# Three moves in the opening lists of an attention and expert kernel: k of two pairs, V's copies and loads, a subtraction

## The chip, the core and the metric

The kernel runs on one core of a Trainium2 chip. A core has five engines, each with an instruction queue of its own that is worked off in order: TensorE (PE in the profile; PEld is its weight load), VectorE (DVE), ScalarE (ACT), GpSimd (POOL) and SyncE (SP, which only requests transfers). Sixteen DMA engines carry out transfers that SyncE, ScalarE and GpSimd request. The metric is the time of one launch on the device in microseconds (us), as the median of several runs.

## What is computed

Block-causal attention of 8 batches with 8 heads, 576 rows, 64 columns, and then a layer of 8 experts of which each row takes one. Cut to what matters here:

```python
scores = (1/sqrt(D)) * q @ k.T                 # q, k, v: 8 x 8 x 576 x 64, float32
scores = where(block_i >= block_j, scores, -1e9)   # blocks of 64 rows
attn = exp(scores - max(scores)); attn /= sum(attn) + 1e-9
x = (attn @ v), as 4608 rows of 512
# second stage: logits = x @ w_gate, argmax, at most `capacity` (80) rows for an expert,
# out[rows] = gate * (relu(x[rows] @ w1[e]) @ w2[e])
```

## The kernel before

The attention works on 32 pairs of heads, two heads of one batch at a time, so that the two fill 128 partitions. A pair goes through these steps, which are methods of `Pair`:

- `load` requests q (on SyncE), `load_k` requests k: four transfers of 72 KB on GpSimd's queue (L577), for pairs 2 and up. `load_v` requests V in three transfers on GpSimd's queue (L587, L590) and two small ones on SyncE's.
- `prep(0)` turns q: VectorE transposes it in blocks of 32 (L623) and GpSimd multiplies the result `T0` by 1/8 (L626). `prep(1)` turns k into `T1`, with no scaling. For pair 0 TensorE does this instead.
- `scores` lets TensorE multiply `T0` and `T1` into PSUM, in three goes: "3" (two PSUM tiles, 512 and 64 columns), "2" (448 and 64) and "10" (320 and 192). The rows by which the prediction counts time are the x8 products of L645.
- `max` takes the negated row maxima on VectorE (L681), `less` subtracts the maxima of the last block there (L685), and `soft` exponentiates on ScalarE (L702, and L694 for the last block).
- `back` turns the exponentials with TensorE (L732, L740), `take` copies them out of PSUM, mostly on ScalarE (L789), `pad` copies V into a tile with zeros (GpSimd, L599), and `values` multiplies with V on TensorE (L781, L759).

The order of all this is written by hand. `TURN` is a list of steps for iteration i; an entry `(d, what, ...)` does step `what` of pair i + d. `OPENING` holds other lists for the iterations -2, -1 and 0; iteration 1 and all later ones took `TURN`. The lists set the order of emission, and so the place of each instruction in its engine's queue. So `scores` "2" of pair 3 is emitted in iteration 2, and the `prep(0)` that feeds it in iteration 1. Buffers: four for q, four for k, four for V, two for each of `T0` and `T1`, four PSUM tiles that go round.

Two more facts that the emission order decides. Where two engines read the same PSUM tile, the one whose read is emitted later waits for the other's. And a transfer requested by GpSimd carries a wait for the landing of the one eight places ahead of it on that queue.

The second stage, from about 290 us, is ordered by a scheduler that works with simulated times; there TensorE multiplies gathered rows with the experts' weights (L1121). Two small products (L1072, L1086) check the choice of rows; a register load of `bad_i` on SyncE reads the outcome.

Of the kernel before, what the change touches and what calls it, by code (L numbers as in the profile page):

```python
# [34 lines left out]
TURN = (  # L35
    (1, "begin"),
    (0, "scores", "3"),
    (-3, "flip"),
    (0, "max", 3, 0),
    (-1, "back", "C"),  # L40
    (1, "scores", "2"),
    (-1, "take", "back", "C"),
    (0, "max", 3, 1),
# [45 lines left out]
OPENING = {  # L89
    -2: (  # L90
        (2, "prep", 0),
        (2, "load_v"),
        (2, "prep", 1),
        (6, "load"),
    ),
    -1: (
        (1, "begin"),
        (1, "scores", "2"),
        (1, "max", 2, 1),
        (1, "max", 2, 0),  # L100
        (1, "max", 4),
        (1, "soft", 2, 1),
        (1, "soft", 2, 0),
        (1, "less"),
        (1, "soft", 4),
        (6, "load"),
    ),
    0: (
        (0, "scores", "3"),
        (0, "max", 3, 1),  # L110
        (0, "max", 3, 0),
        (0, "scores", "10"),
        (1, "prep", 0),
        (1, "prep", 1),
        (3, "load_k"),
        (1, "begin"),
        (1, "scores", "2"),
        (0, "soft", 3, 1),
# [14 lines left out]
        (1, "soft", 4),  # L133
        (2, "prep", 0),
        (1, "load_v"),
        (4, "load_k"),
        (0, "pad"),
        (2, "load_v"),
        (0, "sum"),
# [5 lines left out]
        (0, "take", "back", "A"),  # L145
    ),
}


@with_exitstack  # L150
# [1264 lines left out]
```

## Time and profile before

| what | us |
|---|---|
| median of 3 timed runs | 407.41 (407.29 to 409.0) |
| the profiled execution | 412.18 |
| its span, first to last instruction | 410.5 |
| TensorE busy | 381.6 (93% of the span) |
| VectorE, ScalarE, GpSimd busy | 280.5, 264.8, 253.9 |

A profile shows one execution. The rows further down are of three kinds: lines of its page, groups of waits, and the timeline of one engine, where consecutive instructions of one kind are merged into a row with its start, its length and, in brackets, how long the engine had stood idle before and what ended that.

### The profile page before, as it was taken

The page shows a single profiled execution, that of the slowest core. Times are in us where ns is not written, and L with a number is a line of the kernel's source. Part 1 is how long each engine was busy: PE and PEld are TensorE (multiplying, and loading weights), DVE is VectorE, ACT ScalarE, POOL GpSimd, SP SyncE. Part 2 cuts the span into 40 slices and gives each one's busy share as a digit, 9 for nine tenths or more (in the row PEclk, how much of TensorE's full clock was granted, in tenths as well). Part 3 has the DMA queues.
Part 4 walks back from the last instruction along what each step waited for, and adds up shares of the span by engine and source line. Part 5 has one row for each costly group of instructions (what it writes and reads, how often), then busy time and mean ns, then how long its engine had stood idle before and what let it go on. Part 6 is the DMA issues. An engine that isn't in the chain of part 4 may idle for free.

```text
span 410.5 us, 15557 instructions
## 1 busy us (share of the span) xinstructions
PE 381.6 (93%) x6351; PEld 295.5 (72%) x6351; DVE 280.5 (68%) x651; ACT 264.8 (65%) x700; POOL 253.9 (62%) x440
## 2 busy tenths in 40 slices
PE   7887999999999999999999999999785999999990
PEld 3565777777777776777777776777544999999980
DVE  5774998998998999899899899887652131111120
ACT  2793999899898999999999999987031111110100
POOL 7598786898798798799779978721587010000000
PEclk9996999999999999999999999999998899999996
DMA  9999639879897997998989999996829999899300
GB/s 142 147 159 144 124 87 233 200 157 191 220 193 154 187 218 156 204 212 158 221 187 222 235 263 330 304 322 217 274 84 255 314 301 317 293 324 314 126 19 22
DMA packets 120124, 84.46 MB, mean 206 GB/s; under 512 B 94429, under 2 KB 96477, under 8 KB 120048
## 3 DMA queue, kind: packets, MB, share of 16 engines
q1 hardware_dynamic: 102432, 45.55, 48.4%
q0 software_dynamic: 15808, 37.55, 36.4%
q8 instruction: 52, 0.85, 0.9%
q10 hardware_dynamic: 1808, 0.31, 0.5%
q14 instruction: 24, 0.20, 0.2%
HBM read 63.25 MB, written 20.33 MB: 204 GB/s over the span
## 4 chain that ended last, share of the span: by engine, by line
PE 84%; POOL 4%; issue 3%; DVE 3%; DMA 2%; SPq 1%; ACT 0%; POOLq 0%; ACTq 0%; DVEq 0%
PE sc L645 23%; PE sc L781 21%; PE ps L1121 11%; PE sc L732 10%; PE av L1121 8%; PE sc L403 2%; PE sc L740 2%; PE sc L422 1%; POOL ld L577 1%; POOL vn L590 1%; PE pm L1164 1%; DMA P<-in_k_dram 1%; PE pm L1134 1%; DMA ld<-in_q_dram 1%; PE sc L759 1%
## 5 line engine op out<-in xcount | busy, mean ns | idle before, releaser
L702 ACT ACTIVATE P<-sc,negm 128x448 f32<-128x448 f32 (+3 forms) x256 | 146.0, 584 | 15.7 <-DVE negm L681 12.3
L681 DVE TENSOR_REDUCE negm<-sc 128x1 f32<-128x448 f32 (+4 forms) x224 | 127.0, 616 | 15.2 <-PE sc L652 13.6
L645 PE MATMUL sc<-T,T 64*128 64x64 f32 (+4 forms) x768 | 113.5, 420 | 7.1 <-POOL T L626 6.4
L645 PEld LDWEIGHTS sc<-T,T 64*128 64x128 f32 x768 | 71.8, 190 | 39.3 <-issue 25.3
L577 POOL DMA_DIRECT2D ld<-in_k_dram x120 | 81.9, 688 | 0.1
L789 ACT COPY PT<-sc 128x1024 f32<-128x1024 f32 x63 | 60.8, 1016 | 13.3 <-PE sc L732 12.6
L781 PE MATMUL sc<-PT,vn 128*64 128x128 f32 (+1 forms) x512 | 61.0, 380 | 0.6 <-ACT PT L789 0.6
L1169 POOL DMA_INDIRECT out_dram<-y,si x8 | 7.5, 933 | 77.4 <-DVE y L1165 57.2
L732 PE MATMUL sc<-ident,P 64*128 64x64 f32 x1280 | 53.6, 227 | 0.1
L702 ACT ACTIVATION_READ_ACCUMULATOR P<-sc,negm 128x1 f32 x256 | 53.0, 207 | 0.0
L781 PEld LDWEIGHTS sc<-PT,vn 128*64 128x64 f32 x512 | 33.9, 138 | 23.5 <-issue 22.3
L1121 PE MATMUL ps<-xsT,w 128*64 128x80 f32 x1024 | 43.5, 242 | 4.6 <-issue 4.6
L732 PEld LDWEIGHTS sc<-ident,P 64*128 64x128 f32 x1280 | 45.2, 138 | 3.0 <-ACT P L702 1.0
L623 DVE STREAM_TRANSPOSE T<-ld 128x576 f32<-128x576 f32 x62 | 47.3, 764 | 0.0
L1121 PEld LDWEIGHTS ps<-xsT,w 128*64 128x64 f32 x1024 | 40.3, 143 | 7.2 <-issue 6.6
L626 POOL TENSOR_SCALAR T<-T 128x576 f32<-128x576 f32 x31 | 20.7, 668 | 37.6 <-DVE negm L681 18.7
L590 POOL DMA_DIRECT2D vn<-in_v_dram x64 | 39.8, 628 | 0.2 <-DMA w<-in_moe_w_dram 0.2
L1146 ACT ACTIVATE hT<-ps 128x320 f32<-128x320 f32 x16 | 7.0, 438 | 48.1 <-PE ps L1121 48.1
L1156 DVE COPY yT<-av 128x320 f32<-128x320 f32 x7 | 3.4, 491 | 50.0 <-PE av L1121 50.0
L1121 PE MATMUL av<-hT,w 128*64 128x80 f32 x896 | 32.7, 233 | 0.0
L791 DVE COPY xT<-sc 128x576 f32<-128x576 f32 x32 | 24.0, 750 | 12.0 <-PE sc L759 12.0
L1121 PEld LDWEIGHTS av<-hT,w 128*64 128x64 f32 x896 | 32.0, 137 | 0.0
(191 smaller groups left out, 523.8 us busy)
## 6 DMA issues: line engine op xcount, KB each, us to landing
w<-in_moe_w_dram SPq DMA_DIRECT2D x48, 512.0 KB, 5.4
out_dram<-zero SPq DMA_DIRECT2D x18, 512.0 KB, 8.2
ld<-in_q_dram SPq DMA_DIRECT2D x124, 72.0 KB, 4.1
ld<-in_k_dram POOLq DMA_DIRECT2D x120, 72.0 KB, 4.4
xs<-Y POOLq DMA_DIRECT2D x28, 288.0 KB, 5.5
vn<-in_v_dram POOLq DMA_DIRECT2D x32, 128.0 KB, 5.1
vn<-in_v_dram POOLq DMA_DIRECT2D x64, 64.0 KB, 4.9
w<-in_moe_w_dram POOLq DMA_DIRECT2D x8, 512.0 KB, 9.1
```

Of the source, the lines that this page charges most:

```text
L577: eng.dma_start(self.nat[x][r], (q, k)[x][self.b, self.h0 + h, :, 32 * i:32 * i + 32] .rearrange("(g r) d -> r g d", r=32))
L590: nc.gpsimd.dma_start(self.vn[c * BLK:(c + 1) * BLK, 1], turned[:, :, 1 - c])
L623: nc.vector.transpose(t, self.nat[x].rearrange("p g d -> p (g d)"))
L626: nc.gpsimd.tensor_scalar(t, t, scalar1=SCALE, scalar2=1.0, op0=ALU.mult, op1=ALU.mult)
L645: nc.tensor.matmul(to[h], lhsT=self.T[0][r, q:q + P], rhs=self.T[1][r, k0:k1], start=start, stop=stop)
L681: nc.vector.tensor_reduce(to, src, axis=AX.X, op=ALU.max, negate=True)
L702: nc.scalar.activation(dst, src, AF.Exp, bias=self.negm[0:n, u, h:h + 1], scale=1.0, accum_out=self.bt.sums[0:n, u, self.h0 + h:self.h0 + ...
L732: nc.tensor.transpose(pt[:, c, to(c, n_)], row[u][r, h, k(u, h, j):k(u, h, j) + P], ident[r, r])
L781: nc.tensor.matmul(to, lhsT=lhs, rhs=rhs, start=(n_ == 0), stop=(n_ == len(steps) - 1))
L789: nc.scalar.copy(*self.out.pop((what, x)))
L791: nc.vector.tensor_copy(*self.out.pop((what, x)))
L1121: yield nc.tensor.matmul(dst(b)[64 * c:64 * (c + 1)], lhsT=w_[:, a, col:col + 64], rhs=x_[:, a], start=(a == 0 and b == 0), stop=(a == n - ...
```

## The change

Three lists change. In `OPENING[-1]` the subtraction `less` of pair 0 is emitted ahead of two exponentials that read the same PSUM tile, where it had come behind them. In `OPENING[0]` the request of k of pair 3 goes from behind `prep(1)` of pair 1 to the head of the list, and the request of k of pair 4 from behind V's request of pair 1 to the place that k of pair 3 had. And iteration 1 gets a list of its own: `TURN` with `pad` of pair 1 and `load_v` of pair 3 moved from ahead of `prep(0)` of pair 3 to behind it.

```diff
--- before.py
+++ after.py
@@ -99,20 +99,21 @@
         (1, "max", 2, 1),
         (1, "max", 2, 0),
         (1, "max", 4),
+        (1, "less"),
         (1, "soft", 2, 1),
         (1, "soft", 2, 0),
-        (1, "less"),
         (1, "soft", 4),
         (6, "load"),
     ),
     0: (
+        (3, "load_k"),
         (0, "scores", "3"),
         (0, "max", 3, 1),
         (0, "max", 3, 0),
         (0, "scores", "10"),
         (1, "prep", 0),
         (1, "prep", 1),
-        (3, "load_k"),
+        (4, "load_k"),
         (1, "begin"),
         (1, "scores", "2"),
         (0, "soft", 3, 1),
@@ -133,7 +134,6 @@
         (1, "soft", 4),
         (2, "prep", 0),
         (1, "load_v"),
-        (4, "load_k"),
         (0, "pad"),
         (2, "load_v"),
         (0, "sum"),
@@ -145,6 +145,9 @@
         (0, "take", "back", "A"),
     ),
 }
+_put = [step for step in TURN if step not in ((0, "pad"), (2, "load_v"))]
+_at = _put.index((2, "prep", 0)) + 1
+OPENING[1] = tuple(_put[:_at]) + ((0, "pad"), (2, "load_v")) + tuple(_put[_at:])
 
 
 @with_exitstack
```

On GpSimd's queue, in the opening (`ld1` is k, `vn` V, `T0` q turned; L577 requests k, L626 scales q). Before, `T0_297` being pair 1's:

```order
L369 MEMSET sums_250 64x8
L626 TENSOR_SCALAR T0_297<-T0_297 128x576
L577 DMA ld1_302<-in_k_dram 32x18x32 x4
L626 TENSOR_SCALAR T0_352<-T0_352 128x576
L587 DMA vn_355<-in_v_dram 128x4x64
```

and now:

```order
L372 MEMSET sums_250 64x8
L580 DMA ld1_272<-in_k_dram 32x18x32 x4
L629 TENSOR_SCALAR T0_302<-T0_302 128x576
L580 DMA ld1_307<-in_k_dram 32x18x32 x4
L629 TENSOR_SCALAR T0_357<-T0_357 128x576
```

k of pair 3 (`ld1_302` before, `ld1_272` now) stands ahead of the scaling of pair 1's q, and k of pair 4 has the place that it left.

On the same queue, from there to the scaling of pair 3's q (`T0_486` before, `T0_478` now; L599 is V's copy). Before:

```order
L587 DMA vn_355<-in_v_dram 128x4x64
L590 DMA vn_355<-in_v_dram 64x4x64 x2
L577 DMA ld1_361<-in_k_dram 32x18x32 x4
L599 COPY VZ_133<-vn_222 64x256 x2
L587 DMA vn_368<-in_v_dram 128x4x64
L590 DMA vn_368<-in_v_dram 64x4x64 x2
L577 DMA ld1_394<-in_k_dram 32x18x32 x4
L599 COPY VZ_133<-vn_355 64x256 x2
L587 DMA vn_455<-in_v_dram 128x4x64
L590 DMA vn_455<-in_v_dram 64x4x64 x2
L626 TENSOR_SCALAR T0_486<-T0_486 128x576
```

and now:

```order
L590 DMA vn_360<-in_v_dram 128x4x64
L593 DMA vn_360<-in_v_dram 64x4x64 x2
L602 COPY VZ_133<-vn_222 64x256 x2
L590 DMA vn_368<-in_v_dram 128x4x64
L593 DMA vn_368<-in_v_dram 64x4x64 x2
L580 DMA ld1_394<-in_k_dram 32x18x32 x4
L629 TENSOR_SCALAR T0_478<-T0_478 128x576
L602 COPY VZ_133<-vn_360 64x256 x2
L590 DMA vn_483<-in_v_dram 128x4x64
L593 DMA vn_483<-in_v_dram 64x4x64 x2
```

Between the scalings of pair 2's and of pair 3's q stand four groups (V of pair 1, a copy, V of pair 2, k of pair 5) where there were seven; k of pair 4, the copy of pair 1's V and V of pair 3 no longer stand there.

The queues of VectorE, ScalarE and SyncE keep their order through the attention. On VectorE and ScalarE the waits move: before, the subtraction L685 of pair 0 waited for ScalarE's exponentials; now the first of these waits for the subtraction.

In the second stage the scheduler sets a few instructions otherwise. TensorE, in expert 2's first layer (`ps`<-`xsT`,`w` are its products, `ones` the checking products), before:

```order
L1121 MATMUL ps_5860<-xsT_5617,w_4753 64x80 x13
L1072 LDWEIGHTS ones_110
L1072 MATMUL av_5810<-chk_5802,ones_110 128x10
L1164 MATMUL pm_5850<-ident_79,yT_5766 80x128 x4
L1121 MATMUL ps_5860<-xsT_5617,w_4753 64x80 x19
L1121 MATMUL ps_5894<-xsT_5617,w_4753 64x80 x7
L1086 LDWEIGHTS ones_110
L1086 MATMUL av_5823<-dsb_5819,ones_110 128x1
L1121 MATMUL ps_5894<-xsT_5617,w_4753 64x80 x25
```

and now:

```order
L1124 MATMUL ps_5860<-xsT_5617,w_4753 64x80 x9
L1075 LDWEIGHTS ones_110
L1075 MATMUL av_5810<-chk_5802,ones_110 128x10
L1167 MATMUL pm_5850<-ident_79,yT_5766 80x128 x4
L1124 MATMUL ps_5860<-xsT_5617,w_4753 64x80 x15
L1089 LDWEIGHTS ones_110
L1089 MATMUL av_5823<-dsb_5819,ones_110 128x1
L1124 MATMUL ps_5860<-xsT_5617,w_4753 64x80 x8
L1124 MATMUL ps_5894<-xsT_5617,w_4753 64x80 x32
```

The first checking product stands four products earlier, the second fifteen. On VectorE there, before:

```order
L1109 TENSOR_TENSOR xn_6172<-xg_5452 80x4x64 x2
L1094 TENSOR_SCALAR comb_5495<-ids_5793 80x8
L1056 TENSOR_TENSOR comb_5495<-comb_5495,gsum_5795 80x8
L1074 TENSOR_SCALAR good_5812<-av_5810,iota_p_113,caplt_124 80x8
L1084 TENSOR_REDUCE nb_5821<-av_5810 128x1
L1078 SCALAR_TENSOR_TENSOR dif_5814<-occ_5800,caplt_124,good_5812 80x8
L1165 TENSOR_SCALAR y_5849<-pm_5850,comb_5495 80x512
L1080 TENSOR_REDUCE dsum_5817<-dif_5814 128x1
L1082 SCALAR_TENSOR_TENSOR dsb_5819<-cap_123,dsum_5817 128x1
```

and now:

```order
L1097 TENSOR_SCALAR comb_5495<-ids_5793 80x8
L1059 TENSOR_TENSOR comb_5495<-comb_5495,gsum_5795 80x8
L1112 TENSOR_TENSOR xn_6172<-xg_5452 80x4x64 x2
L1077 TENSOR_SCALAR good_5812<-av_5810,iota_p_113,caplt_124 80x8
L1087 TENSOR_REDUCE nb_5821<-av_5810 128x1
L1081 SCALAR_TENSOR_TENSOR dif_5814<-occ_5800,caplt_124,good_5812 80x8
L1083 TENSOR_REDUCE dsum_5817<-dif_5814 128x1
L1085 SCALAR_TENSOR_TENSOR dsb_5819<-cap_123,dsum_5817 128x1
L1168 TENSOR_SCALAR y_5849<-pm_5850,comb_5495 80x512
```

The scaling of `y` has moved behind `dsb`, which the second checking product reads, and the division `xn` behind two short operations. On SyncE the register load of `bad_i` stands six weight transfers later.

## Rows read from the trace of the kernel before

**Rows 1.** The page's chain of work that ended last: share of the span by engine.

```profile
PE 84%; POOL 4%; issue 3%; DVE 3%; DMA 2%; SPq 1%; ACT 0%; POOLq 0%; ACTq 0%; DVEq 0%
```

**Rows 2.** TensorE's waits, 20 to 45 us: line, releaser, us in total, times, longest.

```profile
PE sc L645 <- POOL T L626: 3.8, 1, 3.8
```

**Rows 3.** Timeline of TensorE: start us, us, line, operation, out<-in, count, [idle before].

```profile
14.87 1.19 PE L645 MATMUL sc<-T,T 64*128 64x448 f32 x8 [1.78 <-POOL T L626]
...
27.42 1.25 PE L645 MATMUL sc<-T,T 64*128 64x512 f32 x8
...
28.80 0.41 PE L740 MATMUL sc<-ident,P 64*128 64x64 f32 x5
33.05 2.18 PE L645 MATMUL sc<-T,T 64*128 64x448 f32 x8 [3.84 <-POOL T L626]
...
35.10 2.06 PE L645 MATMUL sc<-T,T 64*128 64x320 f32 x8
...
41.57 1.25 PE L645 MATMUL sc<-T,T 64*128 64x512 f32 x8
...
43.30 1.19 PE L645 MATMUL sc<-T,T 64*128 64x448 f32 x8
...
49.39 1.25 PE L645 MATMUL sc<-T,T 64*128 64x512 f32 x8
```

**Rows 4.** Busy time of each engine by stretch, granted clock, DMA share, GB/s.

```profile
31.00:33.00 2.00, 0.00 (x0) 0.00 (x0) 0.00 (x0) 0.56 (x2) 1.92 (x5) 0.57 1.18 157
33.00:35.00 2.00, 1.95 (x8) 1.13 (x10) 0.00 (x0) 0.00 (x0) 2.00 (x4) 0.50 1.29 156
...
39.00:41.00 2.00, 2.00 (x50) 1.75 (x48) 1.25 (x5) 1.64 (x8) 1.53 (x3) 1.00 0.56 101
```

**Rows 5.** Timeline of GpSimd, opening, columns as in Rows 3.

```profile
6.02 2.91 POOL L577 DMA_DIRECT2D ld<-in_k_dram  x4
...
14.14 0.68 POOL L626 TENSOR_SCALAR T<-T 128x576 f32<-128x576 f32 x1 [3.04 <-DVE T L623]
...
19.28 0.81 POOL L587 DMA_DIRECT2D vn<-in_v_dram  x1
...
21.32 2.67 POOL L577 DMA_DIRECT2D ld<-in_k_dram  x4
...
26.78 2.66 POOL L577 DMA_DIRECT2D ld<-in_k_dram  x4
29.48 0.84 POOL L599 COPY VZ<-vn 64x256 f32<-64x256 f32 x2
...
32.34 0.66 POOL L626 TENSOR_SCALAR T<-T 128x576 f32<-128x576 f32 x1
32.96 2.73 POOL L577 DMA_DIRECT2D ld<-in_k_dram  x4
```

**Rows 6.** Timeline of VectorE, opening.

```profile
11.65 0.28 DVE L685 TENSOR_TENSOR P<-sc,negm 64x128 f32<-64x128 f32 x1 [1.48 <-ACT P L702]
...
13.18 1.42 DVE L623 STREAM_TRANSPOSE T<-ld 128x576 f32<-128x576 f32 x2
...
24.85 0.77 DVE L623 STREAM_TRANSPOSE T<-ld 128x576 f32<-128x576 f32 x1
...
26.51 0.76 DVE L791 COPY xT<-sc 128x576 f32<-128x576 f32 x1 [0.22 <-PE sc L759]
27.18 0.77 DVE L623 STREAM_TRANSPOSE T<-ld 128x576 f32<-128x576 f32 x1
```

**Rows 7.** Timeline of ScalarE, the copies ahead of pair 3's first product.

```profile
27.12 1.93 ACT L789 COPY PT<-sc 128x1024 f32<-128x1024 f32 x2
```

**Rows 8.** Requests of tile ld, 0 to 50 us: from issue to landing.

```profile
DMA to landing us min/median/max: 4.1/4.7/5.8
```

**Rows 9.** Timeline of TensorE, second stage, up to the second checking product.

```profile
333.86 2.02 PE L1121 MATMUL ps<-xsT,w 128*64 128x80 f32 x52
335.81 0.18 PE L1086 MATMUL av<-dsb,ones 128*128 128x1 bf16 x1
```

**Rows 10.** Timeline of VectorE there, what the second product reads.

```profile
333.97 0.75 DVE L1165 TENSOR_SCALAR y<-pm,comb 80x512 f32<-80x512 f32 x1
...
334.82 0.16 DVE L1082 SCALAR_TENSOR_TENSOR dsb<-cap,dsum 128x1 bf16<-128x1 f32 x1
```

## The prediction

> **What bounds the kernel now.** I read first the chain of work that ended last: TensorE holds 84% of it, every other engine 4% or less [rows 1]. So the question is where TensorE stands still or runs slowly, and whether the change touches that place. The waits of TensorE in the opening hold one that counts, 3.8 us in one piece, for GpSimd's scaling of a turned q [rows 2]. TensorE's timeline places it: the products of pair 2 and the turning of pair 1 end at 28.80 + 0.41 = 29.21, and pair 3's "2" product starts at 33.05, after 3.84 us of nothing [rows 3]. The granted clock falls in that pause, to 0.57 of full speed between 31 and 33 us, and is 0.50, the lower of the two levels (1.2 GHz), between 33 and 35, with TensorE at work again; by 39 us it is back at 1.00 [rows 4]. That product takes until 35.10 there, 2.05 us; the next pair's same rows run at the upper level with 1.19 for the merged row against 2.18 [rows 3].
>
> The price of the whole disturbance is read without splitting it: from one pair's "3" product to the next it is 41.57 - 27.42 = 14.15 us, and in the next, undisturbed turn 49.39 - 41.57 = 7.82 us [rows 3]. That is **6.33 us** too many: 3.84 of pause and 2.49 of slow clock and what hung on it. From 41.57 on the chain is TensorE without a break of this size, so a microsecond won here should reach the end.
>
> **Why GpSimd is late.** GpSimd scales pair 3's q at 32.34 [rows 5], though VectorE had turned it by 24.85 + 0.77 = 25.62 [rows 6]. It is not waiting: from 19.28 on it works through requests of V and k and V's copies, and none of the rows up to there has idle time in brackets.
>
> **The change, part by part.**
>
> *Three groups leave the stretch ahead of that scaling.* k of pair 4 takes from 21.32 for 2.67; the copy of pair 1's V and the request of pair 3's V take from 29.48 to 32.34, 2.86 us [rows 5]. Together 5.53. The scaling then starts at 32.34 - 5.53 = 26.8, behind the transpose (25.62), and ends 0.66 later at 27.5. TensorE wants it at 29.21, so 1.7 us of slack take the place of 3.84 of lateness. What is late next at 29.21? The turned k of pair 3 is there at 27.18 + 0.77 = 27.95 [rows 6]. The PSUM tile is freed by ScalarE's second copy at 27.12 + 1.93 = 29.05 [rows 7]. Both just make it. ScalarE and VectorE then have the lead that they have in an undisturbed turn. So the pause goes, and the clock, whose fall came in the pause, has no reason to fall: -6.33 us.
>
> *What comes behind the scaling.* The groups are not removed; they are now ahead of pair 4's scaling. GpSimd from 26.8: scaling 0.62 (32.34 to 32.96), copy and V 2.86, k of pair 6 2.73, a copy 0.84, V 2.04 (19.28 to 21.32) [rows 5]; that is 35.9, and with its own 0.66 pair 4's scaling ends at 36.6. TensorE will want it at 43.30 - 6.33 = 36.97 [rows 3]. Cover: 0.4 us. After that GpSimd gains on TensorE, since its turn is 0.62 + 2.73 + 0.84 + 2.04 = 6.2 us against 7.82. I cost it at nothing; if the cover is gone, every tenth beyond 0.4 is lost, up to the length of a k group, 2.7 us, less 0.4.
>
> *k of pair 3 in GpSimd's pause.* GpSimd stands idle from 11.10 to 14.14 for VectorE's transpose of pair 1's q; a k group has taken 2.66 to 2.91 us [rows 5]. Put there it ends at 13.8 to 14.0, ahead of 14.14. TensorE's first product of pair 1 hangs on that scaling, after 1.78 us of waiting at 14.87 [rows 3], and all that follows hangs on that product, so lateness here is paid in full. The risk is the wait for landings: the second to fourth request need pair 2's first three, issued between 6.02 and 8.2. Landings took 4.1 to 5.8 us, median 4.7 [rows 8]. Counted from the end of an issue, 5.8 would put the last request at 14.0 to 14.7 and the scaling 0.56 later than now; counted from its start, nothing is held. I take no delay (the median), and keep +0.56.
>
> *The subtraction.* Before, VectorE stood idle 1.48 us until 11.65 for ScalarE's exponentials [rows 6]. Now the subtraction can run at 10.17, and the maxima and transposes behind it move up by as much: pair 1's q is turned at about 12.5 in place of 13.9. The exponentials, now behind the subtraction, start some 0.28 later, its length, but ScalarE waits again for VectorE behind them. Alone this would bring pair 1's scaling forward by 1.4; but k of pair 3 now fills GpSimd until 13.8. What is left is 14.14 - 13.8 = 0.34 us at best. I take 0.1 us of gain for this part and the one before together, from bounds of -0.34 to +0.56.
>
> *k of pair 4 earlier.* It is requested near 14.8 in place of 21.3 and used far behind; no path. It joins transfers in a stretch in which the DMA share is above 1.1 [rows 4], so landings may lengthen; V of pair 1, requested at 19.28 as before, is copied at about 27.4 in place of 29.48, and has six us in place of eight, against a longest landing of 5.8 [rows 8]. SyncE's queue is passed by nothing.
>
> *The second stage.* The second checking product stands 15 products earlier. The 26 products of the list ahead of it are 52 in the trace and took from 333.86 to 335.81, so 75 ns each [rows 9]: it is reached 1.1 us earlier, at 334.7. What it reads ended at 334.82 + 0.16 = 334.98, but 0.67 of that was the scaling of `y` ahead of it, from 333.97 to the next start [rows 10], now behind: 334.3. No wait. The register load is later on a queue in which weights follow; it can hold nothing that it did not hold before. Nought, and at most 0.3 either way.
>
> Sum: -6.33 - 0.1 = **-6.4 us**. The profiled execution's 412.18 would become 405.8 (span 410.5 to 404.1). The median of the timed runs lies 4.77 below the profiled time; the pause is made by the order of one queue, so I take it to be in the timed runs too: 407.41 - 6.4 = **401.0**.
>
> **A rule that speaks against it.** k groups took the same time with VectorE at rest (2.73 at 32.96, VectorE 0.00 busy [rows 4, 5]) as beside a copy out of PSUM and a transpose (2.66 at 26.78 [rows 5, 6]). The Trainium skill, page "SBUF — State Buffer", section "SBUF: two separate sides", says that VectorE in its two-port modes locks GpSimd out, so that a transfer requested there cannot be written out until VectorE is done. By the next section of that page of the Trainium skill a request of about 620 ns then takes some 3100. The rows show no lengthening by what VectorE runs here; a copy from SBUF to SBUF beside a request is not among them.
>
> **Rivals.**
> 1. *Pair 4's scaling becomes the late one.* For: cover of 0.4 us only, landings that can hold a request or V's copy. Against: no such hold in the trace before. A lateness of 1 to 2.5 us costs 0.6 to 2.1: 401.6 to 403.1; as one figure 402.3.
> 2. *The clock is not won back.* The pause goes but another short stop keeps the lower level, or the timed runs never fell to it: only 3.84 is gained: 403.6. Against: the stop of 1.78 us at 14.87 is followed by a product of 1.19, the upper level's length [rows 3].
> 3. *The change does little of what it says in timed runs.* The 4.77 us between profiled and timed could be this very pause, made long by profiling. Then 6.4 - 4.77 = 1.6 is left: 405.8, within 0.5%.
> 4. *Slower: k of pair 3 holds pair 1's scaling.* Its four requests, 0.69 us each in the trace, become long in their new place beside VectorE's transposes. The delay d is paid once, and with a further 2.49 once TensorE's stop of 1.78 there grows to the 3.84 that went with a fallen clock. Break-even is d = 6.33 - 2.49 = 3.84; it is slower by 2.04 us from d = 5.88 on, a group of 3.04 + 5.88 = 8.9 us, 2.2 a request. At 2.3: a group of 9.2, d = 6.16, 407.41 + 6.16 - 3.84 = 409.7. Against: 2.66 to 2.91 for every group, whatever VectorE did [rows 5].
>
> By the 3100 ns of the Trainium skill's page "SBUF — State Buffer" the group would take 12.4 us and the sum would be some 413, an estimate from that page alone.
>
> **How the numbers follow.** Forecast 0.66 (400.3 to 401.6), rival 1 0.13, rival 2 0.09, rival 3 0.08, rival 4 0.04. The range reaches from a gain of 6.33 + 0.34 + 0.3, and 0.2 for the spread of timed runs, 400.2, up to rival 2 with its neighbours, 403.9; it leaves out rivals 3 and 4. A measurement of this kernel can tell about 0.5%, 2.04 us, from no change. Faster by more: forecast and rivals 1 and 2, 0.88; within: rival 3, 0.08; slower: 0.04.
>
> **What would show it.** In the changed profile TensorE's wait for GpSimd of 3.8 us is gone, the granted clock is 1.00 from 29 to 41 us, pair 3's scaling starts near 26.8, pair 4's ends within 0.4 us of TensorE's need, "3" products follow each other by 7.8 us from 27 us on, and the end comes 6.4 us earlier. A k group over 3 us at 11.1, a scaling of pair 1 after 14.2, or a stop of TensorE near 37 us would show steps wrong; an opening shorter by 6 us with an end that is not would show that the chain breaks later.

## The result and the profile of the changed kernel

The changed kernel took 406.39 us, median of eleven runs (403.18 to 408.05); the kernel before took 411.21 in eleven runs taken with them (407.29 to 413.92). The ratio is 0.9893 with a 95% interval of 0.9853 to 0.9934. It was timed three more times in the experiments below, each time beside the kernel before: 0.9832 [0.9777, 0.9887], 0.9859 [0.9801, 0.9917] and 0.9848 [0.9781, 0.9916]. Ratios here and below are taken without the slowest runs of either kernel (over 1.5% above its fastest), so they can differ a little from the quotient of the medians. The four, weighted by the inverse squares of their intervals, give 0.9865 with about 0.0026 either way: 1.35%, or 5.5 us of 411. The forecast was 401.0, a ratio of 0.9843 to the 407.41 from which it set out. So the sign was right, the gain 0.9 us smaller than forecast, and the time itself 2.5 us above the upper end of the range, 403.9, since its starting point was wrong.

The profiled execution took 406.74 us (span 404.9, mean granted clock 0.986); before it was 412.18 (410.5, 0.975).

TensorE's timeline, opening, x8 products of L648 (before L645): start, length, idle before in brackets.

```profile
14.53 1.19 PE L648 MATMUL sc<-T,T 64*128 64x448 f32 x8 [1.41 <-POOL T L629]
...
27.08 1.25 PE L648 MATMUL sc<-T,T 64*128 64x512 f32 x8
...
28.82 1.19 PE L648 MATMUL sc<-T,T 64*128 64x448 f32 x8
...
34.91 1.25 PE L648 MATMUL sc<-T,T 64*128 64x512 f32 x8
...
37.17 1.19 PE L648 MATMUL sc<-T,T 64*128 64x448 f32 x8 [0.47 <-POOL T L629]
...
38.23 1.11 PE L648 MATMUL sc<-T,T 64*128 64x320 f32 x8
...
43.27 1.25 PE L648 MATMUL sc<-T,T 64*128 64x512 f32 x8
```

Against [rows 3]: the pause of 3.84 us ahead of pair 3's "2" product is gone (28.82, no bracket) and the product takes 1.19 in place of 2.05. The next "3" product comes at 34.91 in place of 41.57, 6.66 earlier. One pair on, TensorE waits 0.47, and of the gain 6.12 is left (43.27 against 49.39).

Busy time by stretch, columns as in [rows 4]; the figure third from the end is the granted clock.

```profile
31.00:33.00 2.00, 2.00 (x24) 1.28 (x24) 2.00 (x4) 1.90 (x8) 2.00 (x4) 1.00 0.82 162
33.00:35.00 2.00, 2.00 (x62) 1.93 (x58) 1.75 (x6) 1.87 (x9) 1.90 (x4) 1.00 1.14 151
```

The clock stays at the upper level where it was 0.57 and 0.50. GpSimd's timeline, against [rows 5]:

```profile
11.05 2.67 POOL L580 DMA_DIRECT2D ld<-in_k_dram  x4
13.79 0.68 POOL L629 TENSOR_SCALAR T<-T 128x576 f32<-128x576 f32 x1
...
23.77 1.36 POOL L580 DMA_DIRECT2D ld<-in_k_dram  x2
25.97 1.33 POOL L580 DMA_DIRECT2D ld<-in_k_dram  x2 [0.85 <-DMA vn<-in_v_dram]
27.38 0.66 POOL L629 TENSOR_SCALAR T<-T 128x576 f32<-128x576 f32 x1
28.00 0.84 POOL L602 COPY VZ<-vn 64x256 f32<-64x256 f32 x2
...
36.46 0.67 POOL L629 TENSOR_SCALAR T<-T 128x576 f32<-128x576 f32 x1
```

k of pair 3 fits into the pause (11.05 + 2.67 = 13.72) and pair 1's scaling follows at 13.79. Pair 3's scaling starts at 27.38 in place of 32.34. Ahead of it the third request of k of pair 5 stood still for 0.85 us until a part of V had landed, the transfer eight places ahead on the queue. So pair 4's scaling ends at 37.13, and TensorE, which wanted it at 36.70, waits.

VectorE, with the subtraction ahead of the exponentials (before, 11.65 with 1.48 of waiting, [rows 6]):

```profile
10.24 0.28 DVE L688 TENSOR_TENSOR P<-sc,negm 64x128 f32<-64x128 f32 x1
10.44 1.40 DVE L684 TENSOR_REDUCE negm<-sc 128x1 f32<-128x576 f32 x2
11.77 1.42 DVE L626 STREAM_TRANSPOSE T<-ld 128x576 f32<-128x576 f32 x2
```

From 43 us the two timelines run alike, shifted by 6.12, up to the 29th "3" product at 244.51 (before, 250.63). Then TensorE's timeline shows this:

```profile
244.51 1.25 PE L648 MATMUL sc<-T,T 64*128 64x512 f32 x8
...
249.40 1.20 PE L648 MATMUL sc<-T,T 64*128 64x448 f32 x8 [3.09 <-POOL T L629]
...
250.45 2.06 PE L648 MATMUL sc<-T,T 64*128 64x320 f32 x8
...
257.40 1.30 PE L648 MATMUL sc<-T,T 64*128 64x512 f32 x8
```

It waits 3.09 us for a scaling, and the clock falls behind the wait: the 64x320 product takes 2.06 in place of 1.11. This interval is 12.89 us long where before it was 8.92, with a wait of 0.75. Of the gain 2.15 is left behind it. From the last "3" product to the end of the span the changed kernel's profile is shorter again, 130.02 against 133.46. The experiments show that neither of these two differences can be laid to the change from one profile.

The chain that ended last, share of the span by engine, against [rows 1] with 84% of TensorE and 2% of transfers:

```profile
PE 76%; DMA 10%; POOL 6%; issue 3%; DVE 2%; ACT 0%; POOLq 0%; ACTq 0%; DVEq 0%
```

Of the 10%, 6% are three landings of weights and V between 215 and 244 us, which reach TensorE by way of GpSimd's queue; the rest lies at the start of the second stage, 12.36 us of it in one transfer that ScalarE requested. In the third and fourth profile of the changed kernel the share of transfers is 14% and 4%.

In the second stage TensorE reached the second checking product without a wait, as forecast; what it reads had ended at 326.62 + 0.16 = 326.78.

```profile
327.47 0.18 PE L1089 MATMUL av<-dsb,ones 128*128 128x1 bf16 x1
```

```profile
326.62 0.16 DVE L1085 SCALAR_TENSOR_TENSOR dsb<-cap,dsum 128x1 bf16<-128x1 f32 x1
```

### The profile page after: what moved, and what is told of

The parts are those of the page before. It is cut to its first block, busy times and chain, and to the rows that moved or that the text cites. A ratio compares the mean times of both kernels' runs of the same rounds, so it can differ in the third digit from the quotient of the medians.

```text
span 404.9 us, 15556 instructions
## 1 busy us (share of the span) xinstructions
PE 378.3 (93%) x6351; PEld 292.2 (72%) x6351; DVE 280.9 (69%) x651; ACT 264.6 (65%) x700; POOL 254.3 (63%) x440
## 4 chain that ended last, share of the span: by engine, by line
PE 76%; DMA 10%; POOL 6%; issue 3%; DVE 2%; ACT 0%; POOLq 0%; ACTq 0%; DVEq 0%
PE sc L648 21%; PE sc L784 19%; PE ps L1124 11%; PE sc L735 10%; PE av L1124 8%; DMA vn<-in_v_dram 4%; DMA xs<-rs 3%; DMA w<-in_moe_w_dram 2%; POOL ld L580 2%; PE sc L406 2%; PE sc L743 1%; PE pm L1167 1%; PE sc L425 1%; POOL vn L593 1%; PE pm L1137 1%
## 5 line engine op out<-in xcount | busy, mean ns | idle before, releaser
L648 PE MATMUL sc<-T,T 64*128 64x64 f32 (+4 forms) x768 | 112.5, 417 | 5.7 <-POOL T L629 5.0
L648 PEld LDWEIGHTS sc<-T,T 64*128 64x128 f32 x768 | 71.3, 188 | 37.5 <-issue 24.8
L626 DVE STREAM_TRANSPOSE T<-ld 128x576 f32<-128x576 f32 x62 | 47.3, 765 | 0.0
L1124 PE MATMUL ps<-xsT,w 128*64 128x80 f32 x1024 | 40.1, 234 | 1.4 <-issue 1.4
L1124 PEld LDWEIGHTS ps<-xsT,w 128*64 128x64 f32 x1024 | 37.2, 137 | 3.6 <-issue 2.8
```

Of the source, the lines that this page charges most:

```text
L626: nc.vector.transpose(t, self.nat[x].rearrange("p g d -> p (g d)"))
L648: nc.tensor.matmul(to[h], lhsT=self.T[0][r, q:q + P], rhs=self.T[1][r, k0:k1], start=start, stop=stop)
L1124: yield nc.tensor.matmul(dst(b)[64 * c:64 * (c + 1)], lhsT=w_[:, a, col:col + 64], rhs=x_[:, a], start=(a == 0 and b == 0), stop=(a == n - ...
```

## The experiments

Three readings are taken from every profile: the start of the sixth "3" product (the opening), the interval behind the 29th (the place near 250 us), and the stretch from the last "3" product to the end of the span. What lies between them can be left out: from the sixth "3" product to the 29th all profiles but the two with weights spread take 193.40 to 193.45 us, and from the 30th to the last all twenty take 17.43 to 17.50. An interval is named by the product that ends it: the fourth is the one from the third to the fourth "3" product.

### Both kernels again

Both unchanged, in a later set of runs.

> The kernel before, unchanged, against itself: ratio 1.000. Theory A (the opening's gain of 6.1 us is whole, and what is missing is scatter of places late in the program): its profile repeats the opening to 0.1 us (14.15 us between the third and fourth "3" products, GpSimd wait 3.8 us) and differs from the first profile by up to some us behind 245 us, that is in the products around pair 29 and in the second stage; runs scatter by 2 us or more. Theory B (the later stages give back 1.5 us of the gain by themselves, because they are bound by transfers): the late places of this profile look like those of the first one to about 0.5 us.

> The changed kernel again. Theory A: opening as in its first profile (third to fourth "3" product 7.8 us, a wait of 0.5 us at pair 4), GpSimd's lateness near 245 us another size than 3.1 us, ratio to before 0.985 (6.1 us) within its interval. Theory B: the wait near 245 us is again about 3 us where the kernel before has 0.8, and the ratio is 0.989 (4.5 us).

Measured: the kernel before 410.97 us, 1.0031 [0.9989, 1.0073] of itself; the changed kernel 404.36, 0.9832 [0.9777, 0.9887]. Readings: 56.94, 10.20 and 131.66 before; 51.30, 11.84 and 129.36 changed. At the sixth product both are within 0.3 us of the first pair of profiles. The kernel before came there another way: the clock fell early, behind the stop ahead of pair 1's first product (0.53 of full speed between 17 and 19 us), so its first interval was 10.68 in place of 9.57, and the interval with the pause was 13.30 in place of 14.15. The three runs of 407.29 to 409.0, on which the forecast stood, were the low end of a scatter: they are the three lowest of eleven, the other eight being 409.55 to 413.92, and the profiled 412.18 lies in the midst of these. Three runs picked out of eleven by chance are the three lowest once in 165 times, so they look like a set of their own. Profiling adds nothing that shows: in the eighteen runs of the experiments the profiled execution lies 0.2 us above the median on average, from 3.05 below it to 3.01 above.

### Each part alone

The list of iteration 1 alone:

```diff
+_put = [step for step in TURN if step not in ((0, "pad"), (2, "load_v"))]
+_at = _put.index((2, "prep", 0)) + 1
+OPENING[1] = tuple(_put[:_at]) + ((0, "pad"), (2, "load_v")) + tuple(_put[_at:])
```

> Only V's copy and request behind the scaling of q in iteration 1. By the queue of GpSimd: pair 3's scaling at 29.5 in place of 32.3, so TensorE waits 1.0 us in place of 3.8, with no fall of the clock; pair 4's scaling then ends at 39.2 where TensorE wants it at 38.0, a wait of 1.2; gain 4.05 us at pair 4. If the lateness of pair 3 alone counted (no carrying over to pair 4), 5.3 us.

The requests of k alone (`load_k` of pair 3 to the head of `OPENING[0]`, of pair 4 in its place):

```diff
     0: (
+        (3, "load_k"),
...
-        (3, "load_k"),
+        (4, "load_k"),
...
-        (4, "load_k"),
```

> Only k of pairs 3 and 4 moved. By the queue of GpSimd: pair 3's scaling at 29.7, TensorE waits 1.2 us, no fall of the clock, pair 4's scaling in time, gain 5.1 us; with the list of iteration 1 alone it is more than the whole, so the parts overlap. If the moves were additive, this part would be 6.1 less the 4 of the other, 2 us.

The subtraction alone (`less` of pair 0 ahead of the two `soft` in `OPENING[-1]`):

> Only the subtraction of pair 0 ahead of the two exponentials. VectorE's stop of 1.5 us at 10.2 goes; pair 1's q is turned at 12.5 and scaled from 12.7, since no k request stands ahead of it here, so TensorE's first product of pair 1 starts at 13.5 in place of 14.9. GpSimd's queue and the stop of TensorE at pair 3 move as one: gain 1.3 us, stop and slow clock unchanged. If the exponentials, now behind the subtraction, set the pace, no more than 0.3 us.

Measured: 0.9853 [0.9803, 0.9904], 0.9868 [0.981, 0.9925] and 0.9955 [0.9914, 0.9996]. At the sixth "3" product (57.23 in the first profile of before) they start at 53.75, 54.75 and 56.05: 3.5, 2.5 and 1.2 us earlier, where 4.05, 5.1 and 1.3 had been worked out. The subtraction came out as forecast, and alone it leaves the pause whole (3.80). The other two fell short for causes that the rows show. With the list alone the waits for pair 3's and pair 4's scaling came as worked out, 1.00 and 1.15 us, but TensorE's stop ahead of pair 1's first product, no longer than before (1.78, [rows 3]), was followed by a slow product:

```profile
14.76 1.86 PE L648 MATMUL sc<-T,T 64*128 64x448 f32 x8 [1.78 <-POOL T L629]
```

The granted clock between 15 and 17 us was 0.53 there and 1.00 in the kernel before. The third "3" product came at 28.00 in place of 27.42, and these 0.58 us are what the gain fell short by. It is not the list's doing, since the second profile of the kernel before has such a fall behind the same stop. With the requests alone, k of pair 5 stood still 0.91 us for a landing, pair 3's scaling came at 30.64, and TensorE waited:

```profile
26.30 1.44 POOL L577 DMA_DIRECT2D ld<-in_k_dram  x2 [0.91 <-DMA vn<-in_v_dram]
...
30.64 0.66 POOL L626 TENSOR_SCALAR T<-T 128x576 f32<-128x576 f32 x1
```

```profile
31.36 1.19 PE L645 MATMUL sc<-T,T 64*128 64x448 f32 x8 [2.21 <-POOL T L626]
```

The wait of 2.21 cost 11.74 - 7.83 = 3.91 us in all, since the clock fell to 0.50 between 33 and 35. So no part alone takes the pause away; together they do. My 5.1 for the requests alone had left the landing wait out and the clock with it.

The times do not separate the parts. The list alone and the requests alone stand 6.0 and 5.4 us below the kernel before, with 2.1 and 2.4 either way, about what the whole change gains (5.5 over four sets of runs, 6.9 in this one). That is 2.6 and 3.0 more than their openings show, and what it is was not shown.

### Is the loss near 250 us the new order's? Scaling first in all iterations, weights requested elsewhere

```diff
-OPENING[1] = tuple(_put[:_at]) + ((0, "pad"), (2, "load_v")) + tuple(_put[_at:])
+TURN = tuple(_put[:_at]) + ((0, "pad"), (2, "load_v")) + tuple(_put[_at:])
```

> The changed kernel with V's copy and request behind the scaling of q in every iteration from 1 on, not in iteration 1 alone. Theory G (in the changed kernel some 3 us more than before are lost near pair 29, where GpSimd, held by the landings of weights that it requested, scales q late): the scaling stands 2.9 us earlier there, so the interval that was 12.9 and 11.8 us falls to 8 to 9, and the wait of 0.5 us at pair 4 goes too; 3 to 5 us faster than the changed kernel, about 401. Theory N (the interval near pair 29 is long for another reason, a late k or V, or chance): 0.5 us faster.

Measured: 0.9846 [0.9785, 0.9907]; 51.04, 12.68, 129.38. With the scaling ahead of V's copy and load in every turn the interval stays as long, so the order of these groups is not what makes it, and the 3 to 5 us expected did not come.

The next two spread the sixteen early parts of the weights (ten requests, the last two of four parts each), one in each of iterations 10 to 25 (`EARLY` had 2, 2, 2, 2, 4, 4 in iterations 24 to 29), in the changed kernel and in the one before:

```diff
-    EARLY = {n - 8: 2, n - 7: 2, n - 6: 2, n - 5: 2, n - 4: 4, n - 3: 4}
+    EARLY = {i: 1 for i in range(n - 22, n - 6)}
```

> The changed kernel with the weights that GpSimd requests ahead of the second stage spread, one of 16 parts in each of the iterations 10 to 25, in place of 2 to 4 parts in iterations 24 to 29. Theory G: no landing holds GpSimd near pair 29, that interval falls to 8 to 9 us, 3 to 4 us faster than the changed kernel, and 6 us faster than the kernel before with the same spread. Theory N: the interval stays at 12, no gain, or the holding moves to iterations 10 to 25.

> The kernel before with the same spread of weights. Theory G: its interval near pair 29 falls from 8.9 and 10.2 to 8 to 9, so it gains 0.5 to 2 us, less than the changed kernel does; the two then differ by the 6.1 us of the opening. Theory N: the two differ by what they differ now, 4.5 to 6 us, with the interval near pair 29 as it is.

Measured: 0.9897 [0.9836, 0.9957] and 1.0035 [0.999, 1.008], no better than without the edit. The interval behind the 29th product falls to 8.33 and 8.34, but the loss moves to where the weights are now requested: in the changed kernel four intervals of 9.54 to 11.56, with waits of TensorE for GpSimd's scaling of 1.09, 1.65 and 0.94 us between 190 and 229 us, and in the one before four of 9.97 to 12.24, where other profiles have 8.3 to 8.9. The long interval goes with the requests of weights.

### Fewer transfers near 250 us, and the changed kernel a third time

The 512 KB transfers that set `out` to zero were requested in iterations 5 to 27 without every fourth; now in 4 to 21, one in each.

```diff
-            if 4 <= i < n - 4 and i % 4:
+            if 4 <= i < 4 + nz:
```

> The changed kernel, with the 18 transfers that set out to zero (512 KB each, SyncE) requested in iterations 4 to 21, one in each, in place of iterations 5 to 27 without every fourth. In the changed kernel three of them are requested at 224.9, 234.0 and 237.0 us, in the stretch in which GpSimd's requests stand still for landings of weights, k and V. Theory L (the gain is lost near 250 us because GpSimd's requests wait for landings among too many transfers): without these 1.5 MB in that stretch the interval between 3-products there falls from 11.8 to 12.9 to at most 9.5, TensorE's wait there from 2 to 3 us to under 1, and the time from about 405 to 402 to 403. Theory M (what is lost there depends on the weights' own rate alone; the clears take nothing from it): interval 11.5 or more, time 404.5 or more. If the earlier stretch is spoiled by the closer transfers, intervals between 60 and 200 us grow beyond 7.8 to 8.9.

> The kernel before with the same earlier transfers of zeros. Theory L: the loss of 1 to 2.3 us in the interval near 250 us goes, time 409 to 409.5 against 410.5, and the difference to the changed kernel with the same edit is 6 to 6.5 us, the opening's whole gain. If the difference stays at 4.5 to 5 us, the gain is lost behind 260 us as well.

> The changed kernel once more, beside the two others on the same chip: 404 to 406 us, opening as before (3-products 4 to 6 near 34.9, 43.4, 51.2), interval near 250 us 11 to 13 if the larger loss there belongs to the changed kernel; 9 to 10.5, as in the kernel before, if it was scatter of landings.

Measured: 0.9847 [0.9794, 0.99], 1.0018 [0.9982, 1.0053], 0.9859 [0.9801, 0.9917]. Readings: 51.37, 10.30, 133.73; 57.28, 13.68, 133.72; 51.62, 9.02, 134.16. Taking the zeros out of that stretch made no difference that shows. But two profiles settle another question. In the changed kernel, unchanged:

```profile
247.68 1.19 PE L648 MATMUL sc<-T,T 64*128 64x448 f32 x8 [0.85 <-POOL T L629]
```

and in the kernel before with earlier zeros:

```profile
256.33 1.88 PE L645 MATMUL sc<-T,T 64*128 64x448 f32 x8 [3.78 <-POOL T L626]
```

The changed kernel has the short interval (9.02, as 8.92 in the first profile of before), and the order of before has the longest of all (13.68). So the loss near 250 us is not the change's own: it is there in both, the interval being 0.6 to 5.3 us longer than the 8.34 that later runs show for it without a wait.

### The weights off GpSimd's queue; k of pair 5 behind the scaling

The ten early requests of weights go to SyncE, in the changed kernel and in the one before:

```diff
-            nc.gpsimd.dma_start(w_[:, a], view[:, a])
+            nc.sync.dma_start(w_[:, a], view[:, a])
```

> The changed kernel with the early transfers of weights (ten requests at 215 to 256 us) requested by SyncE in place of GpSimd. Theory W: near 250 us TensorE waits for GpSimd's scaling because requests on GpSimd's queue wait for the landing of weights eight places ahead (landings of 6.5 to 14 us). Then with the weights off this queue the holds fall from 4 to 6 us in all to under 2, pair 28's scaling is in time, the interval is 8.3 to 8.9 in place of 9.0 to 12.9, and the time is 1 to 4 us below the changed kernel's. Rival: the transfers themselves are too slow there (the DMA share is above 1.0), so that the k and V landings hold the queue just as long: interval 9 to 13, time as the changed kernel's. A second rival: SyncE's q requests are held by the weights now and q comes late: a wait for VectorE's transpose appears.

> The kernel before with the same edit. Theory W: interval 8.3 to 8.9, time 1 to 4 us below the kernel before; its difference to the changed kernel with the same edit is the opening's whole gain, 5.6 to 6.1 us as the two traces show it at the sixth 3-product. If the difference is 4.5 or less, something behind the attention gives a part back.

And in the changed kernel, alone and with this edit, k of pair 5 behind pair 3's scaling:

```diff
     0: (
...
-        (5, "load_k"),
...
-OPENING[1] = tuple(_put[:_at]) + ((0, "pad"), (2, "load_v")) + tuple(_put[_at:])
+OPENING[1] = tuple(_put[:_at]) + ((0, "pad"), (2, "load_v"), (4, "load_k")) + tuple(_put[_at:])
+OPENING[2] = tuple(_put[:_at]) + ((0, "pad"), (2, "load_v")) + tuple(_put[_at:])
```

> The changed kernel with k of pair 5 requested behind pair 3's scaling and V's copy and load in iteration 1, and the copy and load moved behind the scaling in iteration 2 as well. If the hold of k of pair 5's request (0.85 to 1.4 us) and the groups ahead of pair 4's scaling are what the opening's gain fell short by, the fourth and fifth intervals are 7.83 both (in the changed kernel 7.83 to 8.16 and 8.36 to 8.58) and the sixth 3-product starts 0.5 to 0.75 earlier, near 50.6. In time that is too little to be told. If the landing wait only moves on to the next pair: as the changed kernel, 51.1 to 51.6.

> The changed kernel with both edits, weights requested by SyncE and k of pair 5 behind the scaling. If both theories hold, the sum: 0.5 to 0.75 in the opening and 1 to 4 near 250 us, 7 to 10 us below the kernel before. If neither, the changed kernel's time, 5 to 6 below.

Measured: weights on SyncE, changed 399.83 us, 0.9753 [0.9673, 0.9833]; before 408.88, 0.996 [0.9915, 1.0006]. k of pair 5 behind the scaling 400.52, 0.9757 [0.9678, 0.9836]; both edits 400.74, 0.9769 [0.9687, 0.9852]. The interval behind the 29th product is 8.34, 8.35 and 8.34 in the three kernels with the weights on SyncE. GpSimd's timeline there, first the changed kernel's (third profile), then the one with the weights on SyncE:

```profile
230.71 0.67 POOL L580 DMA_DIRECT2D ld<-in_k_dram  x1 [0.58 <-DMA w<-in_moe_w_dram]
232.42 1.19 POOL L346 DMA_DIRECT2D w<-in_moe_w_dram  x2 [1.04 <-DMA w<-in_moe_w_dram]
...
239.49 0.68 POOL L580 DMA_DIRECT2D ld<-in_k_dram  x1 [0.29 <-DMA w<-in_moe_w_dram]
241.46 1.32 POOL L389 DMA_DIRECT2D xs<-Y  x2 [1.30 <-DMA w<-in_moe_w_dram]
```

```profile
234.41 0.67 POOL L629 TENSOR_SCALAR T<-T 128x576 f32<-128x576 f32 x1 [2.85 <-DVE T L626]
235.03 2.71 POOL L580 DMA_DIRECT2D ld<-in_k_dram  x4
237.74 1.33 POOL L389 DMA_DIRECT2D xs<-Y  x2
```

In the first, requests stand still until a piece of weights has landed. How long such a landing took is in the rows of line L346 in the first profile of the changed kernel (pieces of 512 KB took 6.5 to 8.7 us, the two of 2 MB 11.0 and 14.0):

```profile
DMA to landing us min/median/max: 6.5/7.8/14.0
```

With the weights on SyncE these brackets are gone (one of 1.23 us, for a landing of k, stays at 242.69, and the scaling behind it is in time), and GpSimd is so far ahead that it waits 2.85 us for VectorE. The second rival, a late q, does not show: the transpose that GpSimd waits for there starts at 233.45, and in the first profile of the changed kernel at 233.42.

So the loss goes with the requests of weights on GpSimd's queue. The edit takes two things off this queue, the waits for landings and the requests' own time, which is some 4.5 us in each profile up to the late scaling. The waits are what differs. From 40 us ahead of the 29th product to the late scaling GpSimd's waits for landings add up to 3.96, 5.21 and 7.09 us in the three profiles of the order of before, and TensorE then waited 0.75, 2.03 and 3.78; in the four of the changed kernel they are 6.14, 5.18, 4.01 and 4.80, and TensorE waited 3.09, 1.99, 0.85 and 1.88. Each time that is 2.9 to 3.3 less. This shows the cause of the scatter near 250 us: waits of GpSimd's queue for landings, beyond some 3 us of cover, in both orders. Of these waits 2.9 to 5.8 us are for weights, the rest for V and k. What they would cost without the requests' own time was not tried.

In time the edit did more in the changed kernel than in the one before, 9.05 us between the two medians, where 5.6 to 6.1 was expected and their profiles differ by 5.1 at the last "3" product (270.31 and 275.44) and by 6.2 in span (397.9 and 404.1). For the kernel before 0.996 is a gain of 1.6 us, with an interval from 3.5 down to none, so the 1 to 4 us expected are neither shown nor ruled out. What its other runs spend (404.9 to 410.18, the profiled one 405.83) was not seen, since one execution is profiled.

k of pair 5 behind the scaling makes the fourth and fifth intervals 7.83 and 7.82, as forecast, but the sixth becomes 8.45, with TensorE waiting 0.55 for pair 5's scaling, and the sixth product starts at 51.15. It was not the landing wait that was passed on, as the expectation had it, but the work: from 27.50 to pair 5's scaling at 44.34 GpSimd stands idle for 0.18 us in all, and eight requests of k in a row take 5.31 of it. That this kernel still came out at 0.9757 is in none of these rows; its stretch behind the last "3" product was 125.49, the shortest seen. The two edits together stand no lower than either alone, though the sum was expected; no changed kernel was timed beside these.

### The three together on one chip

> The changed kernel beside e17 and e18 on the same chip. From the opening alone (sixth 3-product 5.7 us earlier on average in three profiles of each) the time is 5 to 6.5 us below the kernel before; interval near 250 us anywhere from 8.9 to 13.

> The changed kernel with k of pair 5 behind the scaling, once more. Its profile showed no gain at the sixth 3-product (51.15 against 51.09 to 51.62), and 11.66 near 250 us, so it should stand within 2 us of the changed kernel; if it stands 4 or more below it, as the first comparison with the kernel before suggests, the gain is in the second stage and another cause must be looked for.

> The changed kernel with the weights requested by SyncE, once more. By the intervals (8.34 in place of 9.0 to 12.9) 0.7 to 4.5 us below the changed kernel, mean of three profiles 2.9; if nothing, what is gained near 250 us is given back in the second stage, where weights are awaited.

Measured: the changed kernel 409.47 us, 0.9848 [0.9781, 0.9916]; k of pair 5 behind the scaling 405.68, 0.9774 [0.9713, 0.9835]; weights on SyncE 407.52, 0.982 [0.9767, 0.9873]; the kernel before took 413.91 on this chip. Readings: 51.48, 11.67, 133.74; 51.11, 10.49, 130.89; 51.48, 8.34, 133.62. With their first comparisons, weighted as above, the weights on SyncE stand at 0.980 (0.0044 either way) and k of pair 5 at 0.977 (0.0048), against 0.9865 (0.0026) of the changed kernel. The first is 2.7 us better, with an error of some 2, near the 2.9 expected from the interval; the second 4 us, with the same error. By this count both stand below the changed kernel, the weights on SyncE by little more than the error; beside it on one chip (0.982 against 0.9848) the gap is 1.2 us and not clear of the noise. Of the second's 4 us the sixth "3" product accounts for 0.2. What the rest is wasn't settled: its two profiles show 125.49 and 130.89 behind the last "3" product, but that stretch was 129.36 to 134.16 in four profiles of the changed kernel alone.

That stretch can be read further. In seven of the twenty profiles TensorE is stopped four to six times in the first expert's first layer, 3.3 to 4.4 us in all, by nothing that the profile shows ("issue" in the rows), and between 28 and 50 us behind the last "3" product the granted clock is 0.77 to 0.84. The first profile of before is one of them, that of the changed kernel is not. Its timeline, and then the stretch in both, columns as in [rows 4]:

```profile
311.18 0.23 PE L1121 MATMUL ps<-xsT,w 128*64 128x80 f32 x1 [1.11 <-issue]
...
314.03 0.30 PE L1121 MATMUL ps<-xsT,w 128*64 128x80 f32 x2 [1.13 <-issue]
315.46 1.61 PE L1121 MATMUL ps<-xsT,w 128*64 128x80 f32 x19 [1.13 <-issue]
```

```profile
305.00:327.00 22.00, 15.70 (x284) 13.62 (x278) 4.40 (x19) 2.76 (x8) 9.35 (x18) 0.84 0.86 257
```

```profile
303.00:325.00 22.00, 17.46 (x426) 15.74 (x420) 5.15 (x23) 3.33 (x9) 9.85 (x18) 1.00 0.85 252
```

From the last "3" product on, these seven took 133.46 to 134.16 us, one of them 130.89, and the other thirteen 125.49 to 132.29, 4.2 less on average. The stops come in both orders (twice and five times). They go by the set of runs: all six profiles of the two sets in which the kernel before took 413.91 and 415.49 us have them, none of the twelve of the three sets in which it took 409.73 to 411.41. What stops TensorE there was not found.

## Why the prediction was off, step by step

**The base failed.** "I take it to be in the timed runs too: 407.41 - 6.4 = 401.0." The prediction took the 4.77 us between the profiled execution and the timed median for a fixed difference between two kinds of run, and set out from the lower. It was scatter: 407.29 to 413.92 in eleven runs of one kernel, of which the three shown were the lowest, and the median in later sets of runs was 409.7 to 415.5. The stops in the second stage, worth some 4 us, are in the profile of before that the 4.77 rests on; that the three timed runs went without them would fit, but of these there is no trace. With 411.21 as base the same gain gives 404.8, and the range would have been 404.0 to 407.7, with the 406.39 inside. The rival that took this difference for the pause itself, made long by profiling, has nothing for it either: the timed gain of 5.5 us is far above the 1.6 that would have been left.

**The pause and the clock: right in kind, read at the top of their scatter.** 6.33 us were read from two intervals of "3" products. In the changed kernel the fourth product starts 6.66 earlier, 6.32 for the pause and 0.34 for what lies ahead of it (27.08 in place of 27.42); this is the best end, 0.34, of the two parts that were costed at 0.1. In four profiles of the order of before (one with earlier zeros, one with the weights on SyncE) the interval with the pause was 14.15, 13.30, 14.19 and 13.26: the pause was 3.78 to 3.85 each time, but the slow clock behind it cost 1.6 to 2.5, so the term was 5.4 to 6.4. k of pair 3 took 2.67, the subtraction started at 10.24 (forecast 10.17), pair 1's scaling at 13.79 (13.8): the landing risk did not occur there. The slower rival, requests made long by VectorE, fell: the group at 11.05 took 2.67 beside the reductions and transposes of VectorE. The Trainium skill, page "SBUF — State Buffer", section "SBUF: two separate sides", has GpSimd's requests wait behind VectorE's two-port modes; no row here shows that, and a copy from SBUF to SBUF beside a request was again not among them.

**Pair 4's cover: mis-sized.** It was costed at nothing with 0.4 us of cover, "no such hold in the trace before". A hold came: 0.85, 0.95, 1.03 and 1.23 us in the four profiles (and 0.36 more in the third), since k of pair 4, whose four requests lay between, no longer stands between V of pair 1 and k of pair 5, and the latter's third request waits for V's landing. This landing took 6.7 and 6.9 us in the first two profiles, where the prediction counted on 5.8 at most from rows of q and k alone [rows 8]. The fifth interval was 8.36, 8.57, 8.58 and 8.75 in four profiles in place of 7.83, 0.74 on average. This is the first rival in small (0.6 to 2.1), and it makes the opening's gain smaller than forecast: the 29th "3" product started at 250.63, 250.35 and 250.70 in three profiles of the order of before (one with earlier zeros) and at 244.51, 244.71, 245.03 and 244.90 in four of the changed kernel, means 250.56 and 244.79, 5.8 us apart. At the sixth product the four profiles of the order of before above and eight of the changed one, some with edits further back, have means of 56.93 and 51.40, 5.5 apart: 0.5 ahead of the third product, 5.8 for the interval with the pause, less 0.7 for pair 4. The timed gain, 5.5, is this within its error; the times of the parts alone, above, do not fit their openings as well.

**"From 41.57 on the chain is TensorE without a break of this size": failed as a statement, without cost to the mean that could be shown.** Near 250 us a wait of 0.75 was in the profile of before, and I passed over it as small. It is a queue with little cover: in other profiles of both orders it was 0.85 to 3.78 us, and the interval 8.92 to 13.68. Whether the changed kernel has the longer ones more often (8.92 and 10.20 in two profiles of before, 13.68 with earlier zeros; 12.89, 11.84, 9.02 and 11.67 in the changed kernel) stays open. The second stage scatters as well, by the stops shown above.

**The second stage: right,** no wait appeared for the moved checking products.

## What to carry to other kernels

Read the base from as wide a sample as there is: forecast a ratio or a difference, and where a profiled and a timed execution of one kernel differ by more than the gain at stake, take that as scatter until shown otherwise. Several profiles of one kernel, compared stretch by stretch, tell where it scatters: here in three places only. Where a queue of requests also carries work that another engine waits for, count its landing waits when requests move closer together, since a cover of 0.4 us beside landings of 4.1 to 5.8 us [rows 8] is none. A small wait in a stretch of heavy transfers is to be read as the best case of a wide scatter; moving the bulk requests to SyncE's queue, where nothing came late by them, took it away (8.92 to 13.68 us with them on GpSimd's queue, 8.34 or 8.35 in four profiles without).

## What the runs showed of the hardware

The granted clock does not always answer to the same stop in the same way. Ahead of pair 1's first product a stop of 1.78 us was followed by a product of 1.19 (clock 1.00) in the kernel before, and by one of 1.86 (0.53) with the list of iteration 1 alone. Near 250 us the same holds; the first row is from the second profile of before, the other from the second of the changed kernel:

```profile
254.18 1.19 PE L645 MATMUL sc<-T,T 64*128 64x448 f32 x8 [2.03 <-POOL T L626]
```

```profile
248.50 1.96 PE L648 MATMUL sc<-T,T 64*128 64x448 f32 x8 [1.99 <-POOL T L629]
```

The first interval was 10.20 us, the second 11.84, so the fall added 1.6 us to a stop of equal length. And the median of the kernel before differed by 5.8 us from one set of runs to another (409.73 to 415.49), and by 2.5 between two sets on one chip (411.41 and 413.91); the whole gain measured here is 5.5.
